# Linear attention and a squared-relu feed-forward net: batch 0's first products ahead, and scores by whole-array matmuls

## The chip, the cores and the metric

The kernel runs on one core of one Trainium2 chip. The metric is the device time of one execution in microseconds (us). The kernel before takes 479.88 us, the median of 14 runs (479.27 to 481.4).

## The reference

Two parts follow each other. There are 8 batches of 8 heads, 1024 tokens and 64 channels; E and F are 64 x 1024.

```
k_proj = E @ k ; v_proj = F @ v                     # 64 x 64 for each head
attn   = softmax(q @ k_proj.T / 8) @ v_proj         # 1024 x 64 for each head
x      = attn, heads side by side                   # 8192 tokens x 512
h      = relu(x @ w_in)                             # 8192 x 2048
out    = (h * h) @ w_out                            # 8192 x 512
```

Inputs and output are float32. The kernel computes in bf16 with float32 sums.

## The kernel before, in words

**Chunks.** The feed-forward part works on half a batch at a time, 512 tokens, which is called a chunk: (b, 0) and (b, 1). Its transposed input is the tile xT. *First* products are x times w_in, *second* products are h times w_out. Each can be made in two ways. The plain way takes 64 whole-array matmuls of 512 columns for a chunk. The other way splits each matrix into 2 x 2 blocks and makes seven block products in place of eight, by 112 matmuls of 256 columns; it needs sums of blocks on both sides. These are `sum_w_in`, `sum_w_out`, `sum_x` and `sum_h`, additions on VectorE (DVE) that all bear the line of the helper `tt`, L155. The sums of h lie in tiles s12 (two buffers) and s4 (three).

**First products.** `first_cold` and `first_plain` are the plain way (line L494): four matmuls make one column block of h, ScalarE (ACT) takes the relu (L490), DVE squares it. A `Group` is the seven-product way (L657): a quarter of a chunk's columns in steps p1 to p7.

**Second products.** `second_cold` is plain (L500), `second_seven` makes the seven products of one chunk by itself (L554), `second_spread` makes the same seven in small pieces (L577) between the pieces of the groups of the next chunk.

**Attention** of batch b is the class `Attention`. `project` makes k_proj and v_proj (L263, L264). `keep_k` copies k_proj into the tile kp, `transpose_k` turns kp into kT by TensorE, `transpose_k_dma` does it by a transposing DMA on SP's queue. q goes the same two ways into qT: `transpose_q` or `transpose_q_chunk` on TensorE, `transpose_q_dma` on SP's queue (L326). A row of qT holds the 64 channels of one head for an even token in the lower 64 partitions and for an odd one in the upper 64. `scores_mm` therefore uses quarters of the array: four matmuls of 64 x 64, one for each of two heads and each token parity, listed in SCORE_QUADS (L334). `exponentials` follows on ACT, then the sums over the 64 rows, their inverse by a logarithm and an exponential, and the values, which DVE multiplies by the inverse into xT (L439, L414). There are three forms of the sums: `chunk_sums` for half of the tokens and four heads, `sums` and `sums_spread` for all tokens and two pairs of heads; the last lets eight DMAs on SP's queue carry the inverse to its partitions (L398).

**Order.** TensorE's order is written by hand. Generators of products yield after each piece, which is a *step*, and the table `plan`, filled by `at(step, ...)` and `on(step, ...)`, places pieces of attention behind steps. In the kernel before the first run of steps is (0,0) first cold, (0,0) second cold, (0,1) first plain, (0,1) second seven; then comes (1,0) first plain; then a long loop, `both`, in which the groups of one chunk go with the spread second products of the chunk before it, 56 steps for a batch. DVE and ACT take their instructions in an order that the scheduler sets.

**Queues.** All loads from memory, which convert to bf16, are issued by GpSimd (POOL), in order. Stores of the output, the transposing DMAs and the spread inverses are issued by SP, in order. There is one K_sb, one V_sb and one Q_sb buffer and one qT, so the load of a batch waits for the last reader of the batch before. In the kernel before `load_q` in the loop also waits for the `done` of an earlier step of attention (argument `behind`), and `load_kv` for nothing more. Output tiles o_sb have three buffers.

**PSUM.** Four banks (`bank`) rotate; two pairs of banks (`att_psum`) serve attention until the loop, where the second, lent pair goes to the second products.

Of the kernel before, what the change touches and what calls it, by code (L numbers as in the profile page):

```python
# [9 lines left out]
P = 128  # L10
# [9 lines left out]
def kernel(  # L20
# [11 lines left out]
    nc = tc.nc  # L32
# [34 lines left out]
    turn = {"att": 0, "bank": 0, "pairs": 2}  # L67
# [4 lines left out]
    def pair_psum(n):  # L72
        return pair_pools[n].tile([P, 2, TCH], F32, tag="pair", name="ps_att")

    def att_psum():
        turn["att"] += 1
        return pair_psum(turn["att"] % turn["pairs"])

    def bank(shape=(P, 512), dtype=F32, n=None):
        if n is None:  # L80
            turn["bank"] += 1
            n = turn["bank"]
        return psum.tile(list(shape), dtype, tag=f"bank{n % 4}", name="ps_bank")
# [48 lines left out]
    for j, (lo, hi) in enumerate(W_IN_PIECES):  # L132
        t = wpool.tile([P, NCB, (hi - lo) * P], BF16, name=f"w_in_{lo}")
        load(t[:], w_in_view[:, :, lo * P:hi * P])
        for fb in range(lo, hi):
            w_in_at[fb] = (t, fb - lo)
        if j < 2:
            load(V0[:, V_PIECES[j + 1]], tokens(v, 0, h=V_PIECES[j + 1]))
    fn = NFB // WP
    for j in range(WP):  # L140
        if j == WP - 1:
            load(Q0[:, :, 4:8, :], tokens(q, 0, i=slice(4, 8)))
# [37 lines left out]
    def sum_w_in(behind):  # L180
        with tc.issue_after(behind.queued.ins):
            for lo, hi in W_IN_PIECES[:3]:
# [41 lines left out]
    SCORE_QUADS = ((LO, 0, 0, LO), (HI, 0, 1, LO), (LO, 1, 1, HI), (HI, 1, 0, HI))  # L224
    VALUE_QUADS = ((LO, 0, 0, LO), (HI, 0, 1, HI), (HI, 1, 1, LO), (LO, 1, 0, HI))

    class Attention:


        def __init__(self, b):  # L230
# [4 lines left out]
            self.kp = proj_pool.tile([P, H // 2, 2, D], BF16, name="kp")  # L235
            self.kT = proj_pool.tile([P, H // 2, 2, KP], BF16, name="kT")
# [9 lines left out]


        def keep_k(self, ps_k, g, second=None):
            view = ps_k.rearrange("k (h d) -> k h d", d=D)
            rows = (LO, HI)[g]  # L250
            nc.vector.tensor_copy(self.kp[rows, :, 0, :], view)
            (second or nc.vector.tensor_copy)(self.kp[rows, :, 1, :], view)
# [6 lines left out]
        def project(self):  # L259
            ps = att_psum()[:, 0]  # L260
            for i in range(NI):
                f, l = i == 0, i == NI - 1
                nc.tensor.matmul(ps[LO, :], lhsT=ET[:, i, :], rhs=self.K[:, :, i, :], start=f, stop=l)  # L263
                nc.tensor.matmul(ps[HI, :], lhsT=FT[:, i, :], rhs=self.V[:, :, i, :], start=f, stop=l)  # L264
            for g in range(2):
                self.keep_k(ps[LO, g * C // 2:(g + 1) * C // 2], g)
            self.keep_v(ps[HI, :])

        def project_k(self, g):
# [5 lines left out]
            self.keep_k(ps[LO, 0:C // 2], g, nc.scalar.copy if g == 0 else None)  # L275
# [12 lines left out]
        def transpose_k(self, gs=(0, 1)):  # L288
            ps = bank([P, H // 2, 2, KP], BF16)
            rows = slice((LO, HI)[gs[0]].start, (LO, HI)[gs[-1]].stop)  # L290
            g = slice(gs[0], gs[-1] + 1)
            for j in range(H // 2):
                nc.tensor.transpose(
                    ps[:, j, g, :].rearrange("p g k -> p (g k)"),
                    self.kp[rows, j].rearrange("k a d -> k (a d)"), ident[rows, rows]
                )
            nc.vector.tensor_copy(self.kT[:, :, g], ps[:, :, g])

        def transpose_k_dma(self):
            nc.sync.dma_start_transpose(  # L300
                self.kT[:].rearrange("p j g k -> p j (g k)"), self.kp[:].rearrange("p j a d -> p (j a d)")
# [3 lines left out]
        def transpose_q_chunk(self, c, src, hg):  # L305
            ps = bank([P, 4, 2, P], BF16)
            for hh in range(4):
# [5 lines left out]
            nc.vector.tensor_copy(self.qT[:, 4 * hg:4 * hg + 4, 2 * c:2 * c + 2, :], ps[:])  # L313
# [17 lines left out]
        def scores_mm(self, ps, pr, n):  # L331
            for o, par, a, r in SCORE_QUADS:
                h = 2 * pr + a
                nc.tensor.matmul(  # L334
                    ps[o, par], lhsT=self.kT[r, h % 4, h // 4, :], rhs=self.qT[r, h, n, :], start=True, stop=True
                )

        def sums_mm(self, ps, e):
            for o, par, a, r in VALUE_QUADS:
                nc.tensor.matmul(ps[o, par], lhsT=ones[r, :], rhs=e[r, par], start=True, stop=True)  # L340

        def values_mm(self, ps, pr, e):
            for o, par, a, r in VALUE_QUADS:
                nc.tensor.matmul(ps[o, par], lhsT=self.vp[r, 2 * pr + a, :], rhs=e[r, par], start=True, stop=True)
# [17 lines left out]
        def sums(self, pr):  # L362

            ps = att_psum()
            for j in range(2):
                for o, par, a, r in VALUE_QUADS:
                    c = 32 * (2 * a + j)
                    nc.tensor.matmul(
                        ps[c:c + 32, par], lhsT=ones[r, 0:32], rhs=self.e[pr + j][r, par], start=True, stop=True
# [11 lines left out]
        def sums_spread(self, pr):  # L381

            ps = att_psum()
            for j in range(2):
                for o, par, a, r in VALUE_QUADS:
                    c = 32 * (2 * a + j)
                    nc.tensor.matmul(
                        ps[c:c + 32, par], lhsT=ones[r, 0:32], rhs=self.e[pr + j][r, par], start=True, stop=True
# [12 lines left out]
        def values(self, pr, spare=False):  # L401
# [7 lines left out]
            for o, par, a, r in VALUE_QUADS:  # L409
                nc.tensor.matmul(  # L410
                    ps_x[par][o], lhsT=self.vp[r, 2 * pr + a, :], rhs=e[r, par], start=True, stop=True
# [31 lines left out]
    class Chunk:  # L443
# [6 lines left out]
        def h_tile(self, kh, part):  # L450
            if (kh, part) not in self.h:
                self.h[kh, part] = form_pool.tile([P, 2, HF // 2, HC], BF16, name="h", tag="h", bufs=7)
            return self.h[kh, part]

        def sum_x(self):
            self.x_sum = x_pool.tile([P, 4, NCB // 2, HC], BF16, name="x_sum")
# [31 lines left out]
        def square(self, fb, ps):  # L488
            h = self.h_tile(fb // HF, fb % HF // 4)[:, :, fb % 4]
            nc.scalar.activation(h, ps.rearrange("p (a t) -> p a t", a=2), AF.Relu)  # L490
            self.queued = tt(h, h, ALU.mult, h)
# [33 lines left out]
        def first_plain(self, order=tuple(fb for j in range(HF) for fb in (j, HF + j)), sums=True):  # L525
            for n, fb in enumerate(order):
# [3 lines left out]
                self.square(fb, ps)  # L530
# [182 lines left out]
    with tc.manual_schedule(engines={PE}):  # L713
# [60 lines left out]
        at(18, sum_w_in, chunk[0, 0])  # L774
        at(21, att.transpose_q_chunk, 1, Q0, 0)
        at(21, att.transpose_q_chunk, 1, Q0, 1)
        at(21, nxt.load_q)
        at(23, att.chunk_scores, 1, 0)
        at(23, att.chunk_scores, 1, 1)
        at(25, att.sums, 0)  # L780
        at(27, att.chunk_values, 1, 0)
        at(27, att.chunk_values, 1, 1)
        at(28, sum_w_out, att)
        at(28, begin, 2)
        at(36, nxt.project)
        at(36, lambda: atts[2].load_kv())
        at(39, nxt.transpose_q, 0)
        at(39, nxt.transpose_q, 1)
        at(39, nxt.transpose_k)
        at(41, nxt.scores, 0)  # L790
        at(41, nxt.scores, 1)
        at(44, nxt.transpose_q, 2)
        at(44, nxt.transpose_q, 3)
        at(44, lambda: atts[2].load_q())
        at(45, nxt.sums, 0)
        at(47, nxt.scores, 2)
        at(49, nxt.scores, 3)
        at(50, nxt.values, 0)
        at(52, nxt.values, 1)
        at(53, nxt.sums, 2)  # L800
        at(59, nxt.values, 2)
        at(60, nxt.values, 3)
        at(60, chunk[1, 1].sum_x)
        at(61, lambda: atts[2].project())
        at(59, begin, 3)
        at(60, lambda: atts[3].load_kv())
        at(61, lambda: atts[2].transpose_q_dma())
        at(61, lambda: atts[3].load_q())
        run_all(chunk[0, 0].first_cold(), chunk[0, 0].second_cold(), chunk[0, 1].first_plain(), chunk[0, 1].second_seven(*(bank()[:] for _ in range(3))))

        nxt = atts[2]
        at(1, nxt.transpose_k)
        at(3, nxt.scores, 0)
        at(5, nxt.scores, 1)
        at(7, nxt.sums_spread, 0)
        at(9, nxt.scores, 2)
        at(11, nxt.scores, 3)
# [108 lines left out]
```

The softmax here doesn't subtract the row's maximum and nothing guards it: scores larger than these inputs give would overflow.

## Time and profile before

| What | Value |
|---|---|
| Median of 14 runs | 479.88 us |
| The profiled execution, its own time | 481.28 us |
| Span of the profiled program in it | 479.4 us |
| TensorE (PE) busy | 469.4 us, 98% |
| TensorE weight loads (PEld) busy | 352.0 us, 73% |
| VectorE (DVE) busy | 349.3 us, 73% |
| ScalarE (ACT) busy | 286.3 us, 60% |
| GpSimd (POOL) busy | 32.7 us, 7% |
| Granted TensorE clock | 0.999 |
| Matmul instructions in the trace | 4096 |

The span is the time from the first to the last instruction of the program; the time around it belongs to the start and the end of the execution. [...] a matmul's own duration is longer than the time to the start of the next one. [...] Lines are those of the kernel before.

### The profile page before, as it was taken

Reading aid. Unit: us, or ns where it says so; the run is one execution under the profiler, and the core shown is the slowest. Engines: PE = TensorE matmul, PEld = TensorE weight load, DVE = VectorE, ACT = ScalarE, POOL = GpSimd, SP = SyncE. Lnnn points to the kernel's source line nnn. Section 1 sums busy time; section 2 is a strip of 40 time slices with the busy share of each in tenths; the row PEclk is TensorE's granted clock in tenths of the full one; section 3 lists DMA queues with packets and bytes.
Section 4 is the critical chain, followed back from the end, with each engine's and each line's share of the span. In section 5 each row is a group of like instructions: output and inputs, shape, how many; then the busy total and the mean of one; then the engine's idle time right before and its main releaser. Section 6 shows DMA issues by size and latency. Waiting matters only on the chain.

```text
span 479.4 us, 10022 instructions
## 1 busy us (share of the span) xinstructions
PE 469.4 (98%) x4096; PEld 352.0 (73%) x4106; DVE 349.3 (73%) x613; ACT 286.3 (60%) x466; POOL 32.7 (7%) x45
## 2 busy tenths in 40 slices
PE   8999999999999999999999999999999999999996
PEld 3444445637878788887878878787878788888885
DVE  2356898866996679767897579966797678967671
ACT  2564567397557774678546784477736775565641
POOL 7410020200010000100010000100000000000000
PEclk9999999999999999999999999999999999999999
DMA  9999998999949498767949499595911054101012
GB/s 183 204 206 205 224 151 145 171 226 209 178 92 183 107 202 177 124 131 184 177 106 203 91 219 175 93 166 126 223 49 55 23 133 111 67 23 67 24 66 89
DMA packets 80046, 66.98 MB, mean 140 GB/s; under 512 B 30720, under 2 KB 76032, under 8 KB 80000
## 3 DMA queue, kind: packets, MB, share of 16 engines
q0 software_dynamic: 30640, 29.23, 39.2%
q1 hardware_dynamic: 49216, 36.97, 29.7%
q8 instruction: 32, 0.52, 0.5%
q10 hardware_dynamic: 144, 0.13, 0.1%
q14 instruction: 14, 0.11, 0.1%
HBM read 59.24 MB, written 16.78 MB: 159 GB/s over the span
## 4 chain that ended last, share of the span: by engine, by line
PE 81%; DVE 10%; ACT 4%; DMA 3%; issue 1%; SPq 1%; DVEq 0%; ACTq 0%
PE ps_bank L657 32%; PE ps_second L577 31%; PE ps_bank L494 6%; PE ps_att L334 2%; PE ps_second L554 2%; PE ps_att L410 2%; PE ps_att L263 2%; DMA rs<-inv 1%; DVE h L155 1%; DVE xT L414 1%; DMA k_f<-in_k_dram 1%; DVE rs L378 1%; DVE w_in_sum L155 1%; DVE w_out_sum L155 1%; DVE xT L439 1%
## 5 line engine op out<-in xcount | busy, mean ns | idle before, releaser
L155 DVE TENSOR_TENSOR h<-h 128x1024 bf16<-128x1024 bf16 (+1 forms) x182 | 107.9, 616 | 38.9 <-ACT h L667 25.3
L657 PE MATMUL ps_bank<-x_sum,w_in_sum 128*128 128x256 bf16 x624 | 93.9, 273 | 0.0
L657 PEld LDWEIGHTS <-w_in_sum 128*128 128x128 bf16 x832 | 78.7, 98 | 16.2 <-issue 7.5
L577 PEld LDWEIGHTS <-h 128*128 128x128 bf16 x832 | 81.3, 98 | 10.7 <-issue 1.0
L549 ACT COPY u<-ps_bank 128x512 f32<-128x512 f32 x107 | 63.2, 591 | 24.5 <-PE ps_bank L657 21.4
L671 DVE CUSTOM_DVE_ANT_0 h<-ps_bank,u 128x512 bf16<-128x512 f32 x104 | 68.4, 685 | 13.0 <-PE ps_bank L657 12.5
L682 ACT COPY ps_bank<-ps_bank 128x512 f32<-128x512 f32 x52 | 29.7, 570 | 78.6 <-PE ps_bank L657 78.6
L667 ACT ACTIVATE h<-ps_bank 128x512 bf16<-128x512 f32 x104 | 62.9, 605 | 16.4 <-PE ps_bank L657 15.5
L657 PEld LDWEIGHTS <-w_in 128*128 128x128 bf16 x624 | 58.8, 98 | 13.9 <-issue 7.2
L577 PEld LDWEIGHTS <-s 128*128 128x128 bf16 x624 | 61.1, 98 | 7.1
L657 PE MATMUL ps_bank<-xT,w_in 128*128 128x256 bf16 x416 | 62.6, 273 | 0.0
L577 PE MATMUL ps_second<-w_out_sum,s 128*128 128x256 bf16 x416 | 62.4, 273 | 0.0
L577 PE MATMUL ps_second<-w_out_sum,h 128*128 128x256 bf16 x416 | 62.2, 273 | 0.0
L577 PE MATMUL ps_second<-w_out,h 128*128 128x256 bf16 x416 | 60.1, 272 | 0.2
L414 DVE TENSOR_TENSOR xT<-ps_att,rs 128x512 bf16<-128x512 f32 x56 | 36.0, 685 | 16.0 <-PE ps_att L410 16.0
L494 PE MATMUL ps_bank<-xT,w_in 128*128 128x512 bf16 x186 | 44.6, 379 | 2.1 <-DVE xT L439 1.0
L490 ACT ACTIVATE h<-ps_bank 128x512 bf16<-128x512 f32 x48 | 28.1, 605 | 16.1 <-PE ps_bank L494 15.9
L155 DVE TENSOR_TENSOR o_sb<-ps_second,u 128x512 f32<-128x512 f32 x27 | 18.5, 685 | 25.9 <-PE ps_second L577 20.7
L494 PEld LDWEIGHTS <-w_in 128*128 128x128 bf16 x192 | 17.7, 97 | 24.6 <-issue 6.2
L348 ACT ACTIVATE expT<-ps_att 128x1024 bf16<-128x1024 f32 x32 | 32.9, 1036 | 3.0 <-PE ps_att L334 2.6
L657 PE MATMUL ps_bank<-x_sum,w_in 128*128 128x256 bf16 x208 | 31.3, 273 | 0.0
L657 PE MATMUL ps_bank<-xT,w_in_sum 128*128 128x256 bf16 x208 | 31.3, 273 | 0.0
(104 smaller groups left out, 477.5 us busy)
## 6 DMA issues: line engine op xcount, KB each, us to landing
out_dram<-o_sb SPq DMA_DIRECT2D x63, 256.0 KB, 3.2
rs<-inv SPq DMA_DIRECT2D x96, 128.0 KB, 2.6
K_sb<-in_k_dram POOLq DMA_DIRECT2D x7, 1024.0 KB, 10.6
V_sb<-in_v_dram POOLq DMA_DIRECT2D x7, 1024.0 KB, 16.7
Q_sb<-in_q_dram POOLq DMA_DIRECT2D x7, 1024.0 KB, 12.6
w_out<-in_moe_w_out_dram POOLq DMA_DIRECT2D x4, 512.0 KB, 17.9
w_in<-in_moe_w_in_dram POOLq DMA_DIRECT2D x3, 512.0 KB, 14.7
k_f<-in_k_dram SPq DMA_DIRECT2D x1, 512.0 KB, 5.6
```

The costliest lines, as they stand in the source:

```text
L155: return nc.vector.tensor_tensor(out=o, in0=x, in1=y, op=op)
L263: nc.tensor.matmul(ps[LO, :], lhsT=ET[:, i, :], rhs=self.K[:, :, i, :], start=f, stop=l)
L348: self.done = nc.scalar.activation(e[:], ps[:], AF.Exp, scale=SCALE)
L414: self.done = nc.vector.tensor_tensor(out=self.xT[:, pr, :, par], in0=ps_x[par].rearrange("p (c t) -> p c t", c=2), in1=rs[:, par].rearran ...
L490: nc.scalar.activation(h, ps.rearrange("p (a t) -> p a t", a=2), AF.Relu)
L494: nc.tensor.matmul(ps[:], lhsT=w_in_blk(cb, fb), rhs=self.xT[:, cb, self.c].rearrange("p a t -> p (a t)"), start=(cb == 0), stop=(cb == NC ...
L549: nc.scalar.copy(u[:], ps)
L577: nc.tensor.matmul(ps[:, i * HM:(i + 1) * HM], lhsT=self.h_form(n, fb)[:, i * P:(i + 1) * P], rhs=w_out_form(n, fb), start=fresh and i == ...
L657: nc.tensor.matmul(ps[:, j * HC:(j + 1) * HC], lhsT=w_in_form(n, cb, 2 * self.g + j), rhs=self.chunk.x_form(n, cb), start=fresh and j == 0 ...
L667: nc.scalar.activation(self.out(kh, a), ps[:], AF.Relu)
L671: nc.vector._custom_dve(TENSOR_ADD_SAT, out=self.out(kh, a), in0=ps[:], in1=more[:], s0=3.0e38, s1=0.0)
L682: nc.scalar.copy(self.chain[:], self.first[:])
```

## The change

- **Order.** (0,0) first products are followed at once by (0,1) first products, in one run. The second half-chunk of batch 0's attention moves between them, by half-chunk sums and values. Then comes (0,0) second by `second_seven`, with batch 1's attention between its products. The plain first products of (1,0), the `second_cold` of (0,0) and the `second_seven` of (0,1) leave the opening; (1,0) becomes groups and (0,1) becomes spread second products in the loop, which starts a chunk earlier on each side. h tiles have nine buffers for seven, and x_sum takes its buffer from them. Six of the relus' squares of (0,1) go to ACT. The three `sum_w_in` pieces are placed apart.
- **Scores.** kp and kT are single tiles for all batches. kp holds each head's k twice, on the diagonal of a 128 x 128 block whose other half is zero. `scores_mm` makes two whole-array matmuls, one for each head, in place of four quarters. k and v projections go to two banks of the pair. The rows of the exponentials are now ordered by token parity, and VALUE_QUADS follows.
- **Queues.** The rest of batch 0's q is loaded in two pieces ahead of the last two w_in pieces. Batch 1's q comes in two halves. In the loop `load_kv` waits for the transposing DMA of the batch before it, that DMA has eight blocks for four, and the q transpose moves from step 2 to step 26 of a batch. The sums of x of the second chunk move from step 36 to step 51.

```diff
-    SCORE_QUADS = ((LO, 0, 0, LO), (HI, 0, 1, LO), (LO, 1, 1, HI), (HI, 1, 0, HI))
-    VALUE_QUADS = ((LO, 0, 0, LO), (HI, 0, 1, HI), (HI, 1, 1, LO), (LO, 1, 0, HI))
+    kp = const_pool.tile([P, H, 2, D], BF16, name="kp")
+    nc.vector.memset(kp[:], 0.0)
+    kT = const_pool.tile([P, H, 2, KP], BF16, name="kT")
+    VALUE_QUADS = ((LO, 0, 0, LO), (HI, 1, 1, HI), (HI, 0, 1, LO), (LO, 1, 0, HI))
...
         def keep_k(self, ps_k, g, second=None):
             view = ps_k.rearrange("k (h d) -> k h d", d=D)
-            rows = (LO, HI)[g]
-            nc.vector.tensor_copy(self.kp[rows, :, 0, :], view)
-            (second or nc.vector.tensor_copy)(self.kp[rows, :, 1, :], view)
+            nc.vector.tensor_copy(kp[LO, g, 0, :], view)
+            (second or nc.vector.tensor_copy)(kp[HI, g, 1, :], view)
...
         def scores_mm(self, ps, pr, n):
-            for o, par, a, r in SCORE_QUADS:
+            for a in range(2):
                 h = 2 * pr + a
                 nc.tensor.matmul(
-                    ps[o, par], lhsT=self.kT[r, h % 4, h // 4, :], rhs=self.qT[r, h, n, :], start=True, stop=True
+                    ps[:, a], lhsT=kT[:, h].rearrange("p g k -> p (g k)"), rhs=self.qT[:, h, n, :], start=True, stop=True
                 )
...
         def transpose_k_dma(self):
-            nc.sync.dma_start_transpose(
-                self.kT[:].rearrange("p j g k -> p j (g k)"), self.kp[:].rearrange("p j a d -> p (j a d)")
+            self.kT_done = nc.sync.dma_start_transpose(
+                kT[:].rearrange("p h g k -> p h (g k)"), kp[:].rearrange("p h a d -> p (h a d)")
             )
...
-        def square(self, fb, ps):
+        def square(self, fb, ps, on_scalar=False):
             h = self.h_tile(fb // HF, fb % HF // 4)[:, :, fb % 4]
             nc.scalar.activation(h, ps.rearrange("p (a t) -> p a t", a=2), AF.Relu)
-            self.queued = tt(h, h, ALU.mult, h)
+            if on_scalar:
+                nc.scalar.activation(h, h, AF.Square)
+            else:
+                self.queued = tt(h, h, ALU.mult, h)
...
-        run_all(chunk[0, 0].first_cold(), chunk[0, 0].second_cold(), chunk[0, 1].first_plain(), chunk[0, 1].second_seven(*(bank()[:] for _ in range(3))))
...
-        run_all(chunk[1, 0].first_plain())
...
+        at(12, att.chunk_values, 1, 0)
+        at(14, att.chunk_values, 1, 1)
+        for n, step in enumerate((9, 17, 18)):
+            at(step, sum_w_in, chunk[0, int(n > 0)], n)
+        at(18, chunk[0, 0].sum_h, 0)
+        at(20, chunk[0, 0].sum_h, 1)
+        at(22, sum_w_out, chunk[0, 1])
+        at(24, begin, 2)
+        run_all(chunk[0, 0].first_cold(), chunk[0, 1].first_plain(sums=False, on_scalar=(1, 4, 7, 10, 12, 14)))
+
+        base = turn["bank"]
+        banks = [bank(n=base + n)[:] for n in (1, 4, 3)]
+        turn["bank"], turn["step"], turn["att"] = base + 2, 0, 1
+        at(2, nxt.project)
+        at(2, lambda: atts[2].load_kv())
+        at(3, nxt.transpose_q_chunk, 0, None, 0, nc.scalar.copy)
+        at(5, nxt.transpose_k, (0, 1), nc.scalar.copy, True)
...
+        at(10, lambda: atts[2].load_q())
...
+        run_all(chunk[0, 0].second_seven(*banks))
...
-                if (b, c) == (1, 0):
-                        continue
...
+            if b + 2 < B:
+                if b:
+                    on(t + 11, b + 2, "load_q", lambda b=b: atts[b + 1].done)
+                on(t + (26 if b else 32), b + 2, "transpose_q_dma")
+                on(t + (28 if b else 36), b + 2, "project")
+                on(t + (30 if b else 37), b + 2, "transpose_k_dma")
                 if b + 3 < B:
-                    on(t + 32, b + 3, "load_kv")
+                    at(t + (32 if b else 37), begin, b + 3)
+                    on(t + (32 if b else 37), b + 3, "load_kv", lambda b=b: atts[b + 2].kT_done)
```

## The prediction, made before the changed kernel ran

> **What bounds the kernel now.** First the windows, cut where the kernel changes character: the head, the stretch up to the first grouped product (109.7 us), the long loop, the tail. Columns: PE, PEld, DVE, ACT and POOL busy, clock, DMA share.
>
> ```profile
> 0.00:20.40 20.40, 17.56 (x128) 8.37 (x130) 6.04 (x15) 7.82 (x9) 13.34 (x23) 1.00 1.13 191
> 20.40:109.70 89.30, 86.02 (x600) 42.62 (x609) 65.22 (x131) 53.24 (x80) 8.88 (x11) 1.00 1.09 192
> 109.70:475.70 366.00, 365.81 (x3370) 301.04 (x3367) 277.66 (x467) 224.89 (x377) 10.50 (x12) 1.00 0.58 124
> ```
>
> PE fills the loop. Busy PE is not PE at its pace, so I took the pace from PE's timeline (start, length, instructions):
>
> ```profile
> 105.43 4.49 PE L494 MATMUL ps_bank<-xT,w_in 128*128 128x512 bf16 x20
> 109.75 0.60 PE L657 MATMUL ps_bank<-xT,w_in 128*128 128x256 bf16 x4
> ...
> 151.26 0.60 PE L577 MATMUL ps_second<-w_out_sum,s 128*128 128x256 bf16 x4
> 151.79 0.41 PE L334 MATMUL ps_att<-qT,kT 64*64 64x512 bf16 x4
> 152.13 0.61 PE L657 MATMUL ps_bank<-x_sum,w_in 128*128 128x256 bf16 x4
> ```
>
> Start to start, 20 matmuls of 512 columns take 4.32 us, 0.216 each; four of 256 take 0.44, 0.109 each. A set of four quarter-array scores takes 152.13 - 151.26 - 0.44 = 0.44, values and sums likewise. At these prices the loop has no slack: only PE work moves it.
>
> The middle is different. Its PE work: 192 first products L494 41.5; 64 plain second products L500 13.8; 112 products L554 12.2; two projections (58.09 to 59.94, 1.85 each) 3.7; 56 transposes at 0.056 3.1; the rest of batch 0's v projection 1.2; attention sets 9.2. Sum 84.7 of 89.3, so 4.6 us are lost to waits. PE's waits there, the largest:
>
> ```profile
> PE ps_bank L494 <- DVE xT L439: 1.0, 3, 0.4
> PE ps_bank L554 <- DVE h L155: 0.5, 1, 0.5
> PE ps_bank L494 <- DVE qT L323: 0.3, 1, 0.3
> ```
>
> PE waits for DVE, 98% busy from 50 to 70 us. The chain of waits tells the true pace of DVE and ACT:
>
> ```profile
> 55.14 4.21 DVE w_out_sum L155 x7
> ...
> 72.01 0.92 ACT rs L372
> 72.93 0.49 ACT h L490
> ```
>
> A queued 128x1024 sum takes 0.60, not the mean 0.69 of its group; an exponential or logarithm 0.92, a relu 0.49. Squares follow each other in 0.34.
>
> [...] the quarter-array sets begin 0.20 us after the last whole-array start instead of 0.11, and the next whole-array product waits 0.33. [...]
>
> **The change, part by part (PE first).**
> - Batch 0, first half-chunk: second products from 64 x 0.216 = 13.8 to 112 x 0.109 = 12.2. -1.6.
> - Batch 1, first half-chunk: first products likewise. -1.6.
> - Scores: two whole-array matmuls of 512 columns, 0.43, for a set of four, 0.44. The loop passes from L577 to L657 without a gap[...]. 0.0. [...]
> - Sums: batch 0's second half-chunk needs two sets for one, batch 1 four for two: 3 x 0.44 = +1.3. Values by half-chunk, +0.3. Transposes of k: -4 for batch 2, +4 for batch 1, 0.
> PE work: -1.6.
>
> **Head.** kT's copy doubles, 256 columns 0.28 to 512 0.42, twice; scores wait for it there (0.2 before). I take +0.2 (0 to 0.3). Zeroing kp lies in DVE's 3.5 us wait for E.
>
> **Middle, built anew.** From 20.4 (+0.2) to the first group the changed order has 128 first products 27.6; second seven 12.2; projection 1.85; 56 transposes 3.1; v 1.2; half values 0.5; batch 0's second half-chunk 2.6; batch 1's three scores, three sums, two values 3.5. Sum 52.5. Waits: until 27 us nothing differs and before loses 1.7. Then PE's next needs, walked through in each engine's built order:
> - ACT: 32 relus 15.7, six squares, six exponentials or logarithms 5.5. The square of SBUF data is not in the trace; between a relu's 0.5 and 0.6, six make 3 to 3.6. 24 to 25 us in 29: covered by PE's first products; with that cover gone they would show in full.
> - DVE: 26 squares 8.8, four xT products 2.4, two qT copies 1.2, w_in sums 5.1, h sums 4.8, w_out sums 4.8: 27 in 29. In order, the two multiplies that finish xT of the second half-chunk stand behind the squares of columns 10 to 13 and one sum, and those behind ACT. The values end on PE near 39.2, the second half-chunk's first product asks for xT's last block near 41.6, and DVE has it near 42.3: 0.7 lost.
> - The new h sums need the two s12 buffers, free only once product 6 has read them: DVE idles about 2.5 us there, but PE has products 2 and 7 and transposes to run. The q copies arrive 0.5 us before they are needed. I add 0.4.
> - Loads: the rest of q now precedes two w_in pieces and moves them by about 2.6 us, to 29.1 and 31.7 in place of 26.5 and 29.1; columns 8 start at 32.3, 12 at 37. Batch 1's v lands at 53.6, its projection starts near 57. Covered, by 3 us; the POOL queue gets q's second part a place earlier and one issue (0.9 us) more.
> Groups start at 20.4 + 0.2 + 52.5 + 2.8 = 75.9.
>
> **Loop.** It now also holds what used to lie before 109.7: first products 12.2, second products 12.2, batch 1's last five attention sets and batch 2's projection, scores and one sum, 5.7 in all. 30.1 in all. The remaining 369.7 us are as before: 75.9 + 30.1 + 369.7 = 475.7 against 479.4, **-3.7**. The profiled execution took 481.28 around its 479.4; the runs' median is 479.88, so I expect 476.2. A measurement of this kernel tells about 0.2% from nothing.
>
> **What is queued behind the moved steps.** On SP the q transpose moves from step 2 to step 26 of a 56-step batch, three stores and the k transpose behind it; on POOL the k and v loads wait for the k transpose. The DMA answers:
>
> ```profile
> Q_sb<-in_q_dram POOLq DMA_DIRECT2D x7, 1024.0 KB, 12.6
> V_sb<-in_v_dram POOLq DMA_DIRECT2D x7, 1024.0 KB, 16.7
> ```
> ```profile
> L300 SPq DMA_TRANSPOSE kT<-kp x5: 1210/1252/1278, 140.7 to 362.9; - x5
> ...
> DMA to landing us min/median/max: 2.3/10.0/10.3
> ```
>
> A step is 0.99 us. q is issued at 11, lands at 23.6; its transpose issues from 26 to 30.6 (4.6), three stores of 0.4 to 31.8; k is ready about 31.5, twice as many blocks issue in 2.5: 34.3. The landing took 1 us after issue in the one case without loads beside it (365.23), 8.8 in the four with. Now the loads stand behind it: I take 1 to 2, so 36, against scores at 43.6. k and v then start at 36, land at 53, are needed at 83. The stores wait up to 9 us, under three o_sb buffers: the next put is at 37. Batch 2 is tightest: q issued near 70 lands near 81, transposed by 87; k near 90, scores near 93.
>
> **Rivals.**
> 1. DVE or ACT bound the rebuilt middle: at group means (DVE 32 us, ACT 29 in 29) instead of queued paces, and with each in-order wait exposed, 2 to 4 us more. For it: DVE's 98%. Against it: queued paces are measured. Time 478 to 480, at the edge of no change.
> 2. SP's queue delays kT, the slower side. If k's landing stays at 8.8 us or doubles with its size, it comes at 43 to 52 against 43.6. It decides from 43.6 on; six batches each 0.8 us late return the whole gain. At 45.2: six times 1.6, +9.6 - 3.7, near 486; with partial lateness 481 to 484. Against: the trace's only undisturbed case.
> 3. Better: the spread sums lose the q transpose ahead of them on SP, and xT's wait vanishes. Only 0.1 to 1 us is there: 474.5.
>
> **Chances.** Forecast (474.8 to 478) 0.62; rival 1 0.22; rival 2 0.10; rival 3 0.06. 474.0 to 480.2 leaves out rival 2 and a little of the others. Faster: 0.62 + 0.06 + a third of rival 1 = 0.76; same 0.13 from rival 1; slower 0.11.
>
> **What would show it.** Groups start near 76; no PE wait over 0.3 us in the loop; PE waits for xT near 42; [...] kT landing 2 to 4 us after its issue. Wrong if groups start after 79, or PE's waits name kT or qT in the loop.

## The result, and the profile after

The changed kernel takes 475.58 us, the median of 10 runs (474.86 to 476.96); the kernel before took 480.8 us beside it (48 runs). The ratio is 0.990, with a 95% interval of 0.9889 to 0.9915. The forecast was 476.2, 0.6 us more. Its gain of 3.7 was counted from the 479.88 us of the 14 runs of before known then; beside each other the medians differ by 5.2. A ratio here and below leaves out runs over 1.5% above the fastest of their kernel, a median holds them all. The profiled execution has a time of its own of 477.33 us around a span of 475.6.

First the windows of the kernel after, cut at the first product, at the first grouped product and at the end. The columns are those of the windows before: length, then busy PE, PEld, DVE, ACT and POOL with their instructions, granted clock, DMA share, GB/s.

```profile
0.00:20.84 20.84, 17.31 (x121) 9.43 (x124) 6.83 (x16) 7.88 (x9) 13.23 (x23) 0.92 1.12 190
20.84:76.15 55.31, 53.57 (x420) 30.77 (x424) 43.55 (x86) 39.94 (x60) 7.62 (x9) 1.00 1.13 183
76.15:475.60 399.45, 394.77 (x3598) 328.41 (x3607) 297.73 (x493) 248.72 (x415) 13.14 (x15) 1.00 0.63 135
```

The groups start at 76.15; the forecast put them at 75.9. A second profiled execution of the same kernel, from the last experiment, gives the same middle and a different head:

```profile
0.00:18.82 18.82, 16.00 (x120) 8.42 (x123) 6.83 (x16) 7.87 (x9) 12.42 (x22) 1.00 1.12 191
18.82:74.14 55.32, 53.58 (x421) 30.74 (x425) 43.56 (x86) 39.94 (x60) 8.46 (x11) 1.00 1.17 190
74.14:473.20 399.06, 394.69 (x3598) 328.32 (x3607) 297.54 (x493) 248.58 (x415) 13.11 (x15) 1.00 0.63 135
```

| Part | Before | Forecast | After | After, again |
|---|---|---|---|---|
| Start to first product | 20.44 | 20.6 | 20.84 | 18.82 |
| First product to first group | 89.31 | 55.3 | 55.31 | 55.32 |
| First group to end | 369.65 | 399.8 | 399.45 | 399.06 |
| All but the head | 458.96 | 455.1 | 454.76 | 454.38 |
| Span | 479.4 | 475.7 | 475.6 | 473.2 |

The middle is met to the hundredth in two executions. The head is not a property of the kernel alone: with the same instructions it took 20.84 and 18.82 us. In the first, the granted clock was at half from 7.67 to 11.09 us, in the second it was full from 5.1 us on, and the first loads of k and q landed 0.4 to 0.6 us earlier. The 14 profiles of this case divide in the same way: five whose record of a full clock begins between 4.2 and 5.4 us and stays full have heads of 18.8 to 19.8 us, eight whose record begins between 9.2 and 10.5 us have 20.2 to 20.7. So the kernels are best compared without their heads: -4.2 and -4.6, against -3.9 in the forecast.

The scores, in PE's timeline of the kernel after (start, length, instructions):

```profile
96.57 0.60 PE L586 MATMUL ps_second<-w_out_sum,h 128*128 128x256 bf16 x4
97.01 0.59 PE L340 MATMUL ps_att<-qT,kT 128*128 128x512 bf16 x2
97.44 0.60 PE L666 MATMUL ps_bank<-x_sum,w_in_sum 128*128 128x256 bf16 x4
```

From the product before it to the set 0.44, from the set to the next product 0.43: two matmuls of 0.216, and no gap on either side. (A listed length runs past the next start: four matmuls of 256 columns are listed with 0.60 us, and the set starts 0.44 after them.) PE's waits in the kernel after (total, times, longest), the ones beyond the head:

```profile
PE ps_bank L503 <- DVE xT L445: 1.6, 6, 0.3
...
PE ps_att L416 <- ACT inv L397: 0.3, 1, 0.3
PE ps_att L340 <- DVE kT L302: 0.2, 1, 0.2
```

No line names a transposing DMA. Two of the six waits for xT follow the products that start at 41.69 and 42.31 us; the next products start 0.40 and 0.38 late. In the chain that ended last, before and after, DVE's share has gone from 10% to 2%:

```profile
PE 81%; DVE 10%; ACT 4%; DMA 3%; issue 1%; SPq 1%; DVEq 0%; ACTq 0%
```
```profile
PE 91%; ACT 3%; DMA 2%; DVE 2%; SPq 1%; issue 1%; DVEq 0%; ACTq 0%
```

The k transposes (instruction, duration min/median/max, first and last start; then from issue to landing), and the q transposes with the semaphore that SP stands at ahead of them:

```profile
L305 SPq DMA_TRANSPOSE kT<-kp x6: 1238/1280/2049, 88.1 to 359.1; - x6
...
DMA to landing us min/median/max: 2.8/3.1/4.0
```
```profile
L332 SPq EVENT_SEMAPHORE  x6: 17/9240/9683, 83.9 to 342.4; - x6
L332 SPq DMA_TRANSPOSE qT<-Q_sb x6: 3960/4012/4157, 83.9 to 351.0; - x6
```

By the medians eight blocks issue as fast as four did (1.28 us for 1.25), and land 3.1 us after the start of the issue, where four had taken 10.0 beside the loads. In five of the six batches SP stands 8.6 to 9.7 us until q has landed, with stores behind it, and PE shows nothing of it.

### The profile page after: what moved, and what is told of

Same layout as the page of the kernel before. It is cut to its first block, busy times and chain, and to the rows that moved or that the text cites. A ratio compares the mean times of both kernels' runs of the same rounds, so it can differ in the third digit from the quotient of the medians.

```text
span 475.6 us, 10128 instructions
## 1 busy us (share of the span) xinstructions
PE 465.6 (98%) x4136; PEld 368.6 (78%) x4154; DVE 348.1 (73%) x593; ACT 296.5 (62%) x482; POOL 34.0 (7%) x47
## 4 chain that ended last, share of the span: by engine, by line
PE 91%; ACT 3%; DMA 2%; DVE 2%; SPq 1%; issue 1%; DVEq 0%; ACTq 0%
PE ps_bank L666 36%; PE ps_second L586 35%; PE ps_bank L503 4%; PE ps_bank L563 3%; PE ps_att L271 3%; PE ps_att L340 2%; PE ps_second L563 2%; PE ps_att L416 2%; DMA k_f<-in_k_dram 1%; SPq L404 1%; PE ps_bank L315 1%; DVE xT L445 1%; PE ps_att L393 1%; DMA out_dram<-o_sb 1%; PE ps_bank L279 1%
## 5 line engine op out<-in xcount | busy, mean ns | idle before, releaser
L666 PE MATMUL ps_bank<-x_sum,w_in_sum 128*128 128x256 bf16 x672 | 101.1, 273 | 0.1
L666 PEld LDWEIGHTS <-w_in_sum 128*128 128x128 bf16 x896 | 85.4, 98 | 18.9 <-issue 6.3
L586 PEld LDWEIGHTS <-h 128*128 128x128 bf16 x896 | 87.6, 98 | 10.7
L680 DVE CUSTOM_DVE_ANT_0 h<-ps_bank,u 128x512 bf16<-128x512 f32 x112 | 73.8, 685 | 16.2 <-PE ps_bank L666 12.1
L676 ACT ACTIVATE h<-ps_bank 128x512 bf16<-128x512 f32 x112 | 67.9, 606 | 16.7 <-PE ps_bank L666 15.8
L666 PEld LDWEIGHTS <-w_in 128*128 128x128 bf16 x672 | 64.3, 98 | 14.5 <-issue 5.2
L420 DVE TENSOR_TENSOR xT<-ps_att,rs 128x512 bf16<-128x512 f32 x48 | 30.9, 685 | 14.2 <-PE ps_att L416 14.2
L586 PE MATMUL ps_second<-w_out,s 128*128 128x256 bf16 x224 | 33.6, 273 | 0.0
L503 PE MATMUL ps_bank<-xT,w_in 128*128 128x512 bf16 x124 | 29.7, 379 | 2.0 <-DVE xT L445 1.6
L156 DVE TENSOR_TENSOR s<-h 128x1024 bf16<-128x1024 bf16 x32 | 22.0, 692 | 4.5 <-PE ps_second L586 2.7
## 6 DMA issues: line engine op xcount, KB each, us to landing
K_sb<-in_k_dram POOLq DMA_DIRECT2D x7, 1024.0 KB, 10.2
```

The source lines that it names most:

```text
L156: return nc.vector.tensor_tensor(out=o, in0=x, in1=y, op=op)
L420: self.done = nc.vector.tensor_tensor(out=self.xT[:, pr, :, par], in0=ps_x[par].rearrange("p (c t) -> p c t", c=2), in1=rs[:, par].rearran ...
L503: nc.tensor.matmul(ps[:], lhsT=w_in_blk(cb, fb), rhs=self.xT[:, cb, self.c].rearrange("p a t -> p (a t)"), start=(cb == 0), stop=(cb == NC ...
L586: nc.tensor.matmul(ps[:, i * HM:(i + 1) * HM], lhsT=self.h_form(n, fb)[:, i * P:(i + 1) * P], rhs=w_out_form(n, fb), start=fresh and i == ...
L666: nc.tensor.matmul(ps[:, j * HC:(j + 1) * HC], lhsT=w_in_form(n, cb, 2 * self.g + j), rhs=self.chunk.x_form(n, cb), start=fresh and j == 0 ...
L676: nc.scalar.activation(self.out(kh, a), ps[:], AF.Relu)
```

## The experiments

All times are medians beside the kernel before on the same chip, 480.6 to 480.8 us. The theory: the time is PE's work plus the waits of the middle, and the loop stays free of waits because k and v are loaded behind the k transpose. Rival 1 is DVE as the bound of the middle, rival 2 a late kT.

### The whole-array scores alone

The order and the loads are those of before. The shared kp and kT, the k transpose of eight blocks and the projections in two banks come with the scores; the diff shows the scores.

```diff
-            for o, par, a, r in SCORE_QUADS:
+            for a in range(2):
                 h = 2 * pr + a
                 nc.tensor.matmul(
-                    ps[o, par], lhsT=self.kT[r, h % 4, h // 4, :], rhs=self.qT[r, h, n, :], start=True, stop=True
+                    ps[:, a], lhsT=kT[:, h].rearrange("p g k -> p (g k)"), rhs=self.qT[:, h, n, :], start=True, stop=True
                 )
...
```

> The kernel before with the whole-array scores alone: shared kp and kT, eight blocks in the k transpose, the projections in two banks; order and loads as before. Theory: the two matmuls of 0.43 us cost what the four quarters of 0.44 cost, [...] so the time is that of before, within 0.3 us (span near 479.4); the score sets sit 0.43 us from their neighbours. Rival 2 (the larger k transpose lands late beside the loads, which it still has beside it here): PE waits that name kT, and 1 to 5 us more.

Measured: 498.88 us, ratio 1.038 (1.0359 to 1.0408). Rival 2 in full, and more than its price. PE's waits and the landing of the k transposes in this run:

```profile
PE ps_att L330 <- DMA kT<-kp: 11.9, 4, 3.1
```
```profile
DMA to landing us min/median/max: 3.1/14.0/14.2
```

The score sets themselves cost what they should: in the loop 0.44 us from the product before to the set, 0.43 from the set to the next product. But eight blocks beside the loads landed after 14.0 us, four had taken 10.0, and before had little to spare: its first such transpose landed at 150.87, and the scores that read it started at 151.79; in the three batches that follow 0.8 to 1.1 us were left. Four batches wait some 3.0 us each, 11.9 in all. The rest is the clock: with each of the four waits the trace shows TensorE at half its clock for 3.4 us. Of these 13.7 us 0.8 lie inside the waits, and half of the rest is counted as lost, since at half clock the third experiment, below, shows sets of four matmuls of 256 columns 0.86 us apart in place of 0.44: 11.9 + 6.4 = 18.3. From the first grouped product to the end this run is 18.3 longer than before, so the sum closes there. The whole span is 17.9 longer, with a head 1.5 shorter and a middle 1.1 longer; of the 1.1, eight more transposes of k on PE explain 0.45, and the rest stays open.

### The order with the quarter-array scores

```diff
-            for a in range(2):
+            for o, par, a, r in SCORE_QUADS:
...
-                kT[:].rearrange("p h g k -> p h (g k)"), kp[:].rearrange("p h a d -> p (h a d)")
+                self.kT[:].rearrange("p j g k -> p j (g k)"), self.kp[:].rearrange("p j a d -> p (j a d)")
```

> The changed kernel with the quarter-array scores of before (kp and kT for each batch, four blocks in the k transpose); order and loads as changed. Theory: the gain is the order's; the time is that of the changed kernel within 0.3 us, 3.5 us or more below before. If the whole-array scores carry part of the gain, it comes out 1 us or more above the changed kernel.

Measured: 475.86 us, ratio 0.991 (0.9885 to 0.9939). By the medians, 0.3 apart, the gain is the order's. The profiles are less plain: outside the head the order with quarter-array scores gains 3.4 on before, and the changed kernel 0.8 to 1.2 more. This comes in two parts. The middle is 55.07, 0.25 shorter than with whole-array scores, about what four transposes fewer cost (4 x 0.056). The loop is 400.45, 1.0 to 1.4 longer. Of that, some 0.2 is the sets: in the loop a set with its neighbours takes 0.53 + 0.34 + 0.45 = 1.32 in quarters and 0.44 + 0.43 + 0.44 = 1.31 whole, 24 times; and 0.4 is one wait of a second product for ACT that the other kernel does not have. The rest, 0.4 to 0.8, was not found. So most of the gain is the order's, and how much the whole-array scores add, from 0.3 to 1.2, stays open. With the loads behind them, four blocks land in 2.5 us:

```profile
DMA to landing us min/median/max: 2.3/2.5/2.7
```

### The loads no longer behind the k transpose

```diff
-                    on(t + (32 if b else 37), b + 3, "load_kv", lambda b=b: atts[b + 2].kT_done)
+                    on(t + (32 if b else 37), b + 3, "load_kv")
```

> The changed kernel with the loads of k and v in the loop no longer behind the k transpose. Theory: the k transpose again lands about 10 us after its issue, near step 42 to 43 of a batch against scores at 43.6, so it just holds: 0 to 1 us more than the changed kernel. Rival 2: kT is late by 1 to 2 us in each of six batches, PE waits for kT, 5 to 10 us more.

Measured: 507.88 us (499.63 to 508.26), ratio 1.045 (1.04 to 1.0503). One argument less, and the kernel is 32 us slower by the medians, 25 by the fastest runs. The theory's number was wrong here, since it took a landing of 10 us; rival 2's 5 to 10 us were too few. The waits, the landings, and the first of the waits in PE's timeline:

```profile
PE ps_att L340 <- DMA kT<-kp: 21.0, 5, 6.9
```
```profile
DMA to landing us min/median/max: 2.7/14.0/15.3
```
```profile
93.39 0.60 PE L586 MATMUL ps_second<-w_out_sum,s 128*128 128x256 bf16 x4
100.90 0.61 PE L340 MATMUL ps_att<-qT,kT 128*128 128x512 bf16 x1 [6.90 <-DMA kT<-kp]
101.72 1.06 PE L666 MATMUL ps_bank<-x_sum,w_in_sum 128*128 128x256 bf16 x4 [0.22 <-issue]
102.58 1.06 PE L586 MATMUL ps_second<-w_out_sum,h 128*128 128x256 bf16 x4
```

Ahead of the wait four products of 256 columns are listed with 0.60 us, behind it with 1.06, and they start 0.86 apart in place of 0.44. The windows of this kernel name the reason, a granted clock of 0.50 from 98.92 to 105.75:

```profile
98.92:105.75 6.83, 4.63 (x20) 3.15 (x22) 0.00 (x0) 2.10 (x3) 0.00 (x0) 0.50 0.74 138
```

The sum closes. The waits are 21.0. The clock is at half for 6.8, 3.4, 3.4, 3.4 and 6.8 us, 23.9 in all, of which some 4.4 lie inside the waits: half of 19.5 is 9.8. Together 30.8; the span is 30.9 longer (506.5 against 475.6).

### Quarter-array scores, the loads not behind

The order with the quarter-array scores from above, and the same line as in the last diff.

> The changed order with the quarter-array scores (four blocks in a k transpose) and the loads of k and v not behind it. With four blocks beside the loads, before showed a landing of 10.0 us from the issue; the issue is at step 30 to 31, so kT comes at 41 to 42 against scores at 43.6. Theory: the block count is what makes kT late, so within 0.5 us of the same kernel with the loads behind. If the order (a later q transpose on the same queue) is what makes kT late, 5 us more or worse.

Measured: 493.02 us, scattered from 484.75 to 507.69, ratio 1.014 (1.0104 to 1.0183). With four blocks the transposes are late too:

```profile
PE ps_att L344 <- DMA kT<-kp: 19.0, 4, 7.2
```
```profile
DMA to landing us min/median/max: 2.8/13.5/15.5
```

So the block count is not the only cause: in the changed order four blocks, too, took 13.5 us by the median beside the loads. The profiled execution is the slowest of the six (a span of 505.9), so its waits are those of a bad run, not of the median; they and its clock add up as in the last run: 19.0, and 10.2 + 3 x 6.8 us at half clock less 8.3 inside the waits, halved, 11.2; 30.2 against a span 30.2 longer than with the loads behind.

### The same with the q transposes early

```diff
-                if b:
-                    on(t + 11, b + 2, "load_q", lambda b=b: atts[b + 1].done)
-                on(t + (26 if b else 32), b + 2, "transpose_q_dma")
+                on(t + (2 if b else 32), b + 2, "transpose_q_dma")
...
-                    at(t + (32 if b else 37), begin, b + 3)
-                    on(t + (32 if b else 37), b + 3, "load_kv")
+                    at(t + (2 if b else 37), begin, b + 3)
+                    on(t + (11 if b else 38), b + 3, "load_q", lambda b=b: atts[b + 1].done)
+                    on(t + (32 if b else 37), b + 3, "load_kv", *(() if b else (lambda: atts[2].kT_done,)))
```

> The run with quarter-array scores and loads not behind k, with the q transposes put back to step 2 of a batch and q loaded a batch ahead, as before had them; the loads of batch 3 alone stay behind the k transpose. Theory: a k transpose is late because it is issued while the q transpose and the loads are both in flight; with q's transpose away, kT lands about 10 us after its issue and is in time as in before: 476 to 477, no wait for kT over 0.5 us. If the loads alone make it late in the changed order, PE still waits for kT and the time stays over 484.

Measured: 480.85 us, ratio 1.001 (0.9992 to 1.003). The landings are back at those of before, and no wait for kT is left:

```profile
DMA to landing us min/median/max: 2.3/9.6/10.1
```

That part of the theory holds: with four blocks, and with the q transposes out of the way, the k transposes landed in time beside the loads, after 10.1 us at most. The 476 to 477 did not come, because of one new wait:

```profile
PE ps_att L420 <- ACT inv L401: 3.1, 1, 3.1
```

SP's timeline, and the instruction of ACT that PE waited for:

```profile
102.27 5.04 SPq L408 DMA_DIRECT2D rs<-inv  x8
...
110.74 7.43 SPq L336 DMA_TRANSPOSE qT<-Q_sb  x1
118.28 5.76 SPq L408 DMA_DIRECT2D rs<-inv  x8
```
```profile
113.66 1.02 ACT L401 ACTIVATE inv<-ps_att 128x1024 f32<-128x1024 f32 x1 [3.07 <-DMA rs<-inv]
```

ACT starts the logarithm of the next inverse when the last of eight DMAs of the inverse before it has landed, and PE stands for 3.06 us, until 114.73. These are the eight issued from 102.27 on, ahead of the q transpose at 110.74; the eight behind it are issued when the wait is over. So it is not the hold of SP by the q transpose. The second of the eight was late already when it landed at 110.06, 7.2 us after its issue, and the last landed at 113.59, after 6.9; with the q transposes late and the loads behind these took 3.9 and 2.7. Beside them flew loads of batch 3: the edit also brings that batch's q load forward, to 89.67 in place of 116.69, and v landed 24.1 us after its issue in place of 14.1. That these loads made the eight late is argued and was not tested.

The loop is longer by 3.4 than with the q transposes late and the loads behind, the medians differ by 5.0, and the runs scatter from 478.62 to 484.13. This is the price of the whole edit, once, and not of the place of the q transpose alone.

The seven kernels as a table. Landing is from the issue of a k transpose, in us, min/median/max; waits are PE's for kT. Both are those of the profiled execution, which for the fourth kernel took 507.69 us.

| Kernel | Blocks | k, v behind kT | q transpose | Landing | Waits | Median |
|---|---|---|---|---|---|---|
| before | 4 | no | step 2 | 2.3/10.0/10.3 | 0 | 480.8 |
| scores alone | 8 | no | step 2 | 3.1/14.0/14.2 | 11.9 | 498.88 |
| order alone, not behind, q early | 4 | no, but for batch 3 | step 2 | 2.3/9.6/10.1 | 0 | 480.85 |
| order alone, not behind | 4 | no | step 26 | 2.8/13.5/15.5 | 19.0 | 493.02 |
| changed, not behind | 8 | no | step 26 | 2.7/14.0/15.3 | 21.0 | 507.88 |
| order alone | 4 | yes | step 26 | 2.3/2.5/2.7 | 0 | 475.86 |
| changed | 8 | yes | step 26 | 2.8/3.1/4.0 | 0 | 475.58 |

Either of the two, twice the blocks or a late q transpose, went with a median landing beside loads of 14.0 or 13.5 us in place of 10.0, and with 10.0 only 0.8 to 1.1 us had been left in before. Together they took 14.0, little more. Why a late q transpose does this stays open: in some batches q's transpose was still in flight when k's was issued, but one transpose took 14.2 us although q had landed 0.3 us ahead of it.

The clock records also show when a wait costs more than its length. In these traces a record begins at a multiple of 3.413 us from the first one: before has one record at full clock, 137 of these long, and then half clock; the kernel after has one at full clock, one at half, 136 at full and then half clock. Divide a trace into such stretches, and take those outside the head and the tail with the clock full. In 13 of them PE stood idle for 2.02 to 3.41 us in all (the ends of matmuls are modelled, so these are not exact to the hundredth), one for each of the 13 waits for kT, and each time the next stretch was at half clock. In all others, in every profile here, PE stood for 1.98 us or less, and none was followed by half clock. The wait of 3.06 us for an inverse lay across two stretches, 1.24 and 1.82 us in each. An estimate from these figures, for the time outside the head: a wait under 2 us alone leaves the clock full, one over 4 us has over 2 us in one stretch and brings half clock, and between them it depends on where the wait falls.

### The k transposes placed 11 steps later

```diff
-                on(t + (30 if b else 37), b + 2, "transpose_k_dma")
+                on(t + (41 if b else 42), b + 2, "transpose_k_dma")
...
-                    on(t + (32 if b else 37), b + 3, "load_kv", lambda b=b: atts[b + 2].kT_done)
+                    on(t + (41 if b else 42), b + 3, "load_kv", lambda b=b: atts[b + 2].kT_done)
```

> The changed kernel with the k transposes 11 steps later (5 for the first), the loads of k and v still behind them. In the changed kernel kT lands 7.5 us ahead of its scores (3.0 for batch 2), and 11 steps are 10.9 us: kT is late by 3.4 us five times and by 2 once, 19 us of waits with no load beside the transposes. If a wait costs only its length, 19 more than the changed kernel. If TensorE's granted clock falls to half for 3.4 us after each such wait, as the run with the loads not behind k showed, 1.7 more for each: 27 to 30 more.

Measured: 475.44 us, ratio 0.990 (0.9885 to 0.9922), no change at all. The reason is that nothing was moved: the DMAs of SP and of POOL are issued in the same order in both kernels, and kT of batch 3 is issued 61.3 us after the first group, against 61.6. Only TensorE's order is written by hand; a step in the table fixes a place among PE's instructions, and SP's order, set by the scheduler, did not follow it here. The run says nothing on lateness, and its profile is a third one of the changed kernel: a middle of 55.31 again.

### All squares on VectorE

```diff
-        run_all(chunk[0, 0].first_cold(), chunk[0, 1].first_plain(sums=False, on_scalar=(1, 4, 7, 10, 12, 14)))
+        run_all(chunk[0, 0].first_cold(), chunk[0, 1].first_plain(sums=False))
```

> The changed kernel with all squares on VectorE: six times 0.34, 2.0 us more for VectorE in the middle, and some 3 us less for ScalarE. Theory: PE paces the middle and VectorE has 2 us to spare; only what stands ahead of xT moves, so 0 to 0.5 us more, with the wait for xT near 42 us up to 1.3 us. Rival 1 (VectorE bounds the rebuilt middle): 2 us more.

Measured: 475.93 us, ratio 0.991 (0.9885 to 0.9927). The window of the middle:

```profile
19.82:75.33 55.51, 53.75 (x421) 30.64 (x425) 45.37 (x92) 36.92 (x54) 8.19 (x10) 1.00 1.15 186
```

DVE works 1.8 us more than in the changed kernel, 45.37 for 43.55, and the middle is 0.2 longer. ACT works 3.0 us less, 36.92 for 39.94, and the middle is no shorter for it. Rival 1, with its 2 us, is out, and nothing shows ACT as the bound either.

### The second products of (0,0) made the plain way

```diff
-        at(18, chunk[0, 0].sum_h, 0)
-        at(20, chunk[0, 0].sum_h, 1)
...
-        run_all(chunk[0, 0].second_seven(*banks))
+        run_all(chunk[0, 0].second_cold(base + 1, base + 3))
```

> The changed kernel with the second products of (0,0) made the plain way: 64 matmuls of 512 columns, 13.8 us, in place of 112 of 256 columns, 12.2 us; the sums of h for them, 4.8 us of VectorE, go. Theory: 1.6 us more than the changed kernel, less up to 0.4 of small waits that the sums cause. If the sums cost PE more in waits than the seven products save, it comes out no slower.

Measured: 477.67 us, ratio 0.994 (0.9927 to 0.9957), 2.1 above the changed kernel's median.

```profile
20.47:76.94 56.47, 55.57 (x376) 26.07 (x376) 39.21 (x79) 40.66 (x60) 7.61 (x9) 1.00 1.15 185
```

The middle is 1.15 longer. Up to the first second product it is 0.60 shorter, since the sums of h no longer stand ahead of xT on DVE: of the 0.78 late near 42 us 0.18 is left. From there to the first group it is 1.76 longer, the 1.6 of work and 0.16 more.

### The first products of (1,0) made the plain way, in the loop

```diff
+                    if (b, c) == (1, 0):
+                        yield from chunk[1, 0].first_slow()
+                        continue
                     for g in range(4):
                         new = Group(chunk[b, c], g)
...
```

`first_slow` spreads the 16 column blocks over the 28 steps that the four groups had; the sums of x for the groups go with them.

> The changed kernel with the first products of (1,0) made the plain way inside the loop, 16 column blocks spread over the same 28 steps: 64 matmuls of 512 columns, 13.8 us, in place of 112 of 256 columns, 12.2 us. Theory: 1.6 us more between the first grouped product and the end than the changed kernel's 395.6. If the groups cost waits that the plain way does not have, less than that.

Measured: 480.28 us, ratio 0.999 (0.9978 to 1.0002), 3.9 above the changed kernel on the same chip (476.39, below): the gain is gone. From the first second product of the loop:

```profile
76.42:478.70 402.28, 395.55 (x3543) 323.26 (x3555) 292.51 (x489) 246.63 (x409) 13.10 (x15) 1.00 0.63 133
```

402.28 against 398.57 in the changed kernel (475.60 - 77.03), 3.7 more. The last product starts 2.3 later: 1.6 of work, and one new wait.

```profile
PE ps_att L340 <- PE ps_second L601: 0.6, 1, 0.6
```

The other 1.4 lie behind the last product, where the last store's issue took 2.04 us in place of 0.37. Why stays open, so this run agrees with the 1.6 of work, and does not show how much of the 3.7 is the step's own.

### Batch 0's second values a step earlier

```diff
-        at(12, att.chunk_values, 1, 0)
-        at(14, att.chunk_values, 1, 1)
+        at(11, att.chunk_values, 1, 0)
+        at(13, att.chunk_values, 1, 1)
```

> The changed kernel with the values of batch 0's second half-chunk behind steps 11 and 13 in place of 12 and 14, so that VectorE meets the multiplies into xT ahead of the squares and the sum that stood before them. Theory: the two waits for xT near 42 us, 0.78 together, go or shrink to 0.3: 0.4 to 0.8 us less. Rival: the inverse is not ready, VectorE stands at the multiply and the squares behind it make PE wait elsewhere: no gain or 0.5 more.

> The kernel with batch 0's second values a step earlier once more: 0.8 us less between the first product and the first grouped product than the changed kernel's 55.3, and a median 0.5 to 0.8 us below it.

> The changed kernel itself once more, for comparison with the next run on the same chip: 475.6, 0.990 of before.

Measured: 475.43 us, ratio 0.991 (0.9881 to 0.994), and in the second comparison 475.68 us, ratio 0.988 (0.986 to 0.9899), beside 476.39, 0.990 (0.9883 to 0.9916), for the changed kernel on the same chip. The window of the middle, in the first and in the second profile:

```profile
19.07:73.60 54.53, 53.67 (x424) 30.76 (x424) 43.55 (x86) 39.94 (x60) 8.35 (x10) 1.00 1.18 192
```
```profile
20.64:75.17 54.53, 53.24 (x420) 30.79 (x424) 43.55 (x86) 39.94 (x60) 7.83 (x10) 1.00 1.14 187
```

54.53 twice, against 55.31, 55.32 and 55.31: 0.78 less, the two waits for xT to the hundredth. DVE's timeline of the changed kernel around them, then of this one, whose head is 1.8 us shorter:

```profile
39.81 0.91 DVE L156 TENSOR_TENSOR h<-h 128x512 bf16<-128x512 bf16 x2 [0.40 <-ACT h L496]
40.63 0.69 DVE L156 TENSOR_TENSOR s<-h 128x1024 bf16<-128x1024 bf16 x1
41.24 0.42 DVE L156 TENSOR_TENSOR h<-h 128x512 bf16<-128x512 bf16 x1
41.57 1.28 DVE L445 TENSOR_TENSOR xT<-ps_att,rs 128x512 bf16<-128x512 f32 x2
```
```profile
38.87 0.68 DVE L445 TENSOR_TENSOR xT<-ps_att,rs 128x512 bf16<-128x512 f32 x1
39.47 0.42 DVE L156 TENSOR_TENSOR h<-h 128x512 bf16<-128x512 bf16 x1
39.81 0.69 DVE L156 TENSOR_TENSOR s<-h 128x1024 bf16<-128x1024 bf16 x1
```

The sum s now comes behind the last multiply into xT, not ahead of it. By the trace this is the best version, 0.8 us under the changed kernel. The medians are 0.15 and 0.7 lower, and the intervals overlap: the heads scatter by more than that.

## Why the prediction was right, and where it was not

**Pace and PE work.** 0.216, 0.109 and 0.44 carried the sum. The prediction gives PE's work twice, and the two do not agree: -1.6 part by part, but -2.1 by its rebuilt sums, 52.5 and 30.1 us for 84.7. The forecast rests on the second, with 2.8 us of waits for 4.6. The -1.6 of (0,0)'s second products shows as 1.15 when undone: 1.76 in the second products themselves, less 0.60 of waits that their sums of h cause; the -1.6 of (1,0)'s first products is inside what its undoing cost.

**Scores, 0.0.** Right for the set, 1.31 with its neighbours for 1.32. For the kernel it holds by the medians, 0.3 apart; by the profiles 0.25 are paid in the middle and 1.0 to 1.4 saved in the loop, which the step did not see.

**Head, +0.2.** The step treated as fixed what varies by 2 us with the clock: one kernel's head took 18.82 and 20.84. Among the eight profiles with a full clock from 9.2 to 10.5 us on, four heads with whole-array scores took 20.24 to 20.72 and four with quarters 20.17 to 20.44. The means are 0.2 apart, but the heads overlap, so 0.2 is not contradicted and not shown.

**Middle.** Forecast 55.3, measured 55.31 to 55.32. Walking DVE's built order found the wait for xT, 0.7, measured 0.78, and taking it away gave 0.78. The 0.4 for the sums of h shows as no wait of PE behind 43 us, so the last tenths of the agreement are luck.

**Loop.** 399.8 forecast, 399.45 and 399.06 measured. The 0.3 to 0.7 too much is where the gain outside the head became -4.2 to -4.6 in place of -3.9. That it was so near is in part luck. The 369.7 "as before" belongs to quarter-array scores, and the order with these has a loop of 400.45, 0.65 more than forecast; the whole-array scores, booked at 0.0, took 1.0 to 1.4 back.

**Queues.** The outcome was right and one term was mis-sized. The issue of eight blocks was taken as 2.5, twice that of four, and is 1.28. The landing of 1 to 2 us after the end of the issue is 1.8 (3.1 - 1.28). kT of batch 3 landed at 140.76 against scores at 148.74. SP's stand of up to 9 us was measured as 8.6 to 9.7 and cost nothing.

**Rival 1** fell with the squares on VectorE: 0.2 in place of 2.

**Rival 2** named the right danger and the right guard, and its price was far too low. It had the lateness and left out what a wait of that length does to TensorE. Twelve of the thirteen waits for kT in three kernels were 2.9 to 7.2 us long and one 2.75, and each brought 3.4 to 10.2 us at half clock; a stretch of 3.413 us with no more than 2.02 us of idle time in it was enough. The step "six times 1.6" should have read: the lateness, and 1.6 to 2.8 us on top of each wait (6.4 for four waits, 9.8 for five, 11.2 for four). That is 18 to 31 us for 12 to 21 of waits.

**Rival 3** took a vanished wait for xT as its gain; the change kept the wait, and the shift of one step shows that its 0.8 could be had. Its other half, the q transpose out of the way of the spread inverses, was not tested by itself: in the run with q early PE waited for inverses whose DMAs were issued ahead of the q transpose.

## What to carry to other kernels

Before a transfer is made larger or moved, look for its slack at the reader: before's k transposes had 0.8 to 1.1 us beside the loads, and what kept the change from losing 25 to 32 us is one dependency that holds other loads back until the transposes are through. Price a wait of TensorE of about 3 us in a busy loop at its length and the half-clock time that it can bring, 1.6 us or more for each wait in the three kernels that had them; the waits under 1 us in the middle and the loop here cost their length alone. And where only one engine's order is written by hand, follow the built order of the other queues, for a step in the table need not move them and does not tell when they issue.

## What the runs showed of the hardware

- A transposing DMA of 4 or 8 blocks of 128 x 128 landed 2.5 or 3.1 us after the start of its issue, by the medians, with the loads held back, and beside two loads of 1024 KB after medians of 9.6 to 14.0 us, 15.5 at most. Four blocks held SP for 1.2 to 1.7 us, eight for 1.2 to 2.1 with the loads held back and for up to 4.0 beside them.
- Outside the head and the tail, 13 of 13 stretches of 3.413 us at full clock with 2.02 us or more of idle TensorE were followed by half clock, and none with 1.98 us or less. In the head one stretch with 1.41 us of idle time was followed by half clock too; why stays open.
- At half clock (0.50 from 98.92 to 105.75 us in the kernel with the loads not behind) sets of four matmuls of 256 columns started 0.86 us apart in place of 0.44.
- Whole-array score sets of two matmuls of 512 columns started 0.44 us after the product before them, four matmuls of 256 columns at 0.109 each, and the next product 0.43 after them: 0.216 for each matmul and no gap. Quarter-array sets started 0.09 us late, 0.53 after the product before them, and a set with its neighbours took 1.32 us for 1.31.
- The start of an execution varied by 2 us for one and the same kernel (20.84 and 18.82), and with it when the clock became full: 18.8 to 19.8 us where it was full from 4.2 to 5.4 us on, 20.2 to 20.7 where from 9.2 to 10.5.
